# Attention loads on 128 and 96 partitions, and the second expert's lower parts on VectorE alone

## The chip, the cores and the metric

The kernel runs on one core of a Trainium2 chip. The metric is device microseconds of one execution. TensorE (PE) multiplies matrices from SBUF into PSUM, VectorE (DVE) and ScalarE (ACT) work element by element, GpSimd (POOL) does element work too and issues the gathers and scatters, and SyncE (SP) issues the plain loads and stores. All of these issue into the same 16 DMA engines. TensorE's clock is granted at one of two levels; the profile shows it as 1.00 (2.4 GHz) or 0.50 (1.2 GHz).

## The reference, cut to what matters

```
x = attention(q, k, v)             # 4 batches, 8 heads, 576 positions, head width 64, fp32
    # heads 0..3: a window of the last 32 positions
    # heads 4..7: the last 128 positions, every 4th of them
x = moe(x, ...)                    # 2304 rows of 512; 8 experts, each row goes to its best two
    # h = relu(x @ w1[e]); out += weight * (h @ w2[e]);  w1: 512x1024, w2: 1024x512
return moe2(x, ...)                # the same shapes, each row goes to its best expert
```

## The kernel before

**Attention.** The host has brought the heads into two halves: `half` 0 holds heads 0 to 3 on partitions 0 to 63 of q and k (head width on the partitions), `half` 1 heads 4 to 7 on partitions 64 to 127. Positions are cut into 9 blocks of 64 per half and batch. A "bank" is a pair of blocks: 4 pairs of half 1, one mixed pair of the two last blocks, 4 pairs of half 0, so 9 banks per batch and 36 in all. Loop L1030 does one bank per turn and is skewed: in turn i TensorE does the scores of bank i (L862), the values of bank i-2 (L909), the closing transposes of bank i-3 (L924) and the transposes of the probabilities of bank i-1 (L897). VectorE writes each bank's result to a tile `xo` (L921), of which there are 3; SyncE stores it to `x1` in DRAM (L938, L943). So `xo` of bank 3 can be written once the store of bank 0 has landed. v is held with 96 positions per block: 64 of its own on partitions 32 to 95 and the last 32 of the block before on partitions 0 to 31, each with a load of its own (`load_v`, L825).

SyncE issues all attention loads and stores in program order: batch 0 at L972, batch b+1 while batch b is worked on (L1064 to L1081), as loads of one half of q or k (64 partitions) each. Zeros for the array `x2`, into which the first MoE accumulates, are stored in three pieces in turns 22, 26 and 30 (L950, L1074).

**Weights.** Products of the MoE layers are made from a high part `whi` and a lower part `wlo` of every weight. `load_piece` (L184) loads 1 MB into `raw` (two buffers), ScalarE rounds it to `whi` (L208), and `wlo = raw - whi` (L209) is made in four instructions of 128x512: those with even number on VectorE, the others on the engine `eng`. `eng` is VectorE everywhere but for w1 and w2 of the second expert (L1292 with si = 0, L1268 with si = 1), where it is GpSimd. (The first expert's w1 is made by GpSimd alone, L1084.) While these run, VectorE also does the last part of the first routing (L992, L993), and `xh` and `xl`, the two parts of the second expert's 384 gathered rows (L711 on ScalarE, L712 on VectorE), in three steps from PSUM tiles t, x and q. TensorE's first product of the second expert needs all of `xh` and `whi`, its second all of `xl`.

Within attention the order on VectorE and ScalarE is as written; behind it the framework's scheduler sets it. TensorE's order is as written everywhere.

Of the kernel before, what the change touches and what calls it, by code (L numbers as in the profile page):

```python
# [7 lines left out]
F32 = mybir.dt.float32  # L8
# [9 lines left out]
P = 128  # L18
QB, KB = 64, 96
# [15 lines left out]
Z_AT = (22, 26, 30)  # L35
# [26 lines left out]
def attention_moe_moe_kernel(  # L62
# [5 lines left out]
    nc = tc.nc  # L68
    B, D2, H4, S = q.shape
    D, H = D2 // 2, 2 * H4  # L70
    N, DM = out.shape
    E, _, F = m1_w1.shape
# [139 lines left out]
    def load_w(ring, w, n_out, eng=nc.vector, cuts=1, after=None, all_on=None):  # L212

        ps = []
        per = 2048 // n_out
        for c in range(w.shape[0] // (per * P)):
            hi, lo = load_piece(ring, w[c * per * P:(c + 1) * per * P, :].rearrange("(c p) f -> p c f", p=P), eng, cuts, after, all_on)
            for u in range(per):
                ps.append((hi[:, u * n_out:(u + 1) * n_out], lo[:, u * n_out:(u + 1) * n_out]))
        return ps  # L220
# [575 lines left out]
    with ExitStack() as actx:  # L796
# [6 lines left out]
        KP = KB - QB  # L803
        qs = [ak.tile([P, HH, S], F32, name=f"q{i}") for i in range(2)]
        ks = [ak.tile([P, HH, KP + S], F32, name=f"k{i}") for i in range(2)]
        vs = [ak.tile([P, NB, HH * D], F32, name=f"v{i}") for i in range(3)]
        for k_ in ks:
            nc.vector.memset(k_[:, :, :KP], 0.0)
        for v_ in vs:
            nc.vector.memset(v_[:KP, 0], 0.0)  # L810
        zero = ak.tile([P, P], F32, name="zero")
        nc.vector.memset(zero, 0.0)

        def load_q(b, half, c0=0, c1=S):
            o = half * D
            return qs[b % 2][o:o + D, :, c0:c1], q[b, o:o + D, :, c0:c1]

        def load_k(b, half, c0=0, c1=S):
            o = half * D
            return ks[b % 2][o:o + D, :, KP + c0:KP + c1], k[b, o:o + D, :, c0:c1]  # L820

        def v_of(b, half):
            return vs[(2 * b + 1 - half) % 3]
# [1 line left out]
        def load_v(b, half, j0=0, j1=NB):  # L825

            vb = v_of(b, half)
            src = v[b, half].rearrange("(j p) d -> p j d", p=QB)
            f = max(j0, 1)
            return [(vb[KP:KB, j0:j1], src[:, j0:j1]),  # L830
                    (vb[:KP, f:j1], src[QB - KP:, f - 1:j1 - 1])]


        S4 = S // 4
# [110 lines left out]

        r1 = Route(2, E * cap1 // P, max(r for _, r in regs1), nat, late1)
        n_dyn1 = dyn_tiles(2 * N + sum(r for _, r in regs1), N + r1.pad, rows1)
        ZROWS = -(-(N + P) // (32 * len(Z_AT))) * 32

        def zeros(r0, n):  # L950
            return (x2[r0:r0 + n].rearrange("r d -> (r d)").rearrange("(p c d) -> p c d", p=P, d=P),
                    zero[:, None, :].to_broadcast([P, n * DM // P // P, P]))

        b_tiles = [(b + 1) * S // P for b in range(B)]
        last_pe, last_st = [None], [None]
# [1 line left out]
        def issue(loads):  # L957
            for dst, src in loads:
                nc.sync.dma_start(dst, src)
# [5 lines left out]
        def busy(n, after=None):  # L965

            with tc.issue_after(after) if after is not None else ExitStack():
                for _ in range(n):
                    nc.tensor.matmul(warm, one.to_broadcast([P, P]), one.to_broadcast([P, 224]), start=True, stop=True)

        busy(WARM)
        issue([load_k(0, 1, 0, KB), load_q(0, 1, 0, P), *load_v(0, 1, 0, 2), load_k(0, 1, KB, S), load_q(0, 1, P, S),  # L972
               *load_v(0, 1, 2), load_k(0, 0), load_q(0, 0), *load_v(0, 0)])
        for dst, a, b_ in ((wg1, m1_wg, m1_wn), (wg2, m2_wg, m2_wo)):
            nc.gpsimd.dma_start(dst[:, :, 0, :], a.rearrange("(c p) e -> p c e", p=P))
            nc.gpsimd.dma_start(dst[:, :, 1, :], b_.rearrange("(c p) e -> p c e", p=P))
# [53 lines left out]
        for i in range(len(all_banks) + to_f):  # L1030
            bi = i % n_bi
            if i < len(all_banks):
                bk = Bank()
                bk.b, bk.bi, bk.blocks = all_banks[i]
                queue.insert(0, bk)
                scores(bk)
                if i < len(WARM_1):
                    busy(WARM_1[i], last_pe[0])
            else:
                queue.insert(0, None)  # L1040
            if len(queue) > to_v and queue[to_v]:
                values(queue[to_v])
            if ready:
                logits_part(*ready.pop())
                go_on()
            if len(queue) > to_f:
                bk = queue.pop()
                if bk.bi == 0:
                    xT = ak.tile([P, DC, S], F32, name="xT")
                    if bk.b % 2 == 0:  # L1050
                        lgT = ak.tile([G, 2 * S], F32, name="lgT")
                bk.xT = xT
                finish(bk)
                half, j = bk.blocks[1]
                if half == 0:
                    c0, c1 = (j - 1) * QB, S if bk.bi == n_bi - 1 else (j + 1) * QB
                    ready.append((bk.b, c0, c1 - c0, xT, lgT))
            if len(queue) > to_t and queue[to_t]:
                transposes(queue[to_t])
            if i >= E0_AT and 0 in first_x:  # L1060
                first_products(E0_N)

            if i < len(all_banks):
                if bi == 0:  # L1064
                    more = [[] for _ in range(n_bi)]
                    b = i // n_bi + 1
                    if b < B:
                        for h in (1, 0):
                            f = 0 if h else 4
                            more[f].append(load_k(b, h))  # L1070
                            more[f + 1].append(load_q(b, h))
                            more[f + 2] += load_v(b, h, 0, 4)
                            more[f + 3] += load_v(b, h, 4)
                if i in Z_AT:  # L1074
                    z0 = Z_AT.index(i) * ZROWS
                    more[bi].append(zeros(z0, min(ZROWS, N + P - z0)))
                if last_st[0] is None:
                    issue(more[bi])
                else:
                    with tc.issue_after(last_st[0]):  # L1080
                        issue(more[bi])  # L1081
            if i == W1_AT:
                with tc.issue_after(last_st[0]):
                    w_1 = load_w(wr1, m1_w1[0], F, nc.gpsimd, 4, None, nc.gpsimd)  # L1084
# [163 lines left out]
    def w2_of(role):  # L1248
        if role not in by_load:
            return m1_w2[role]  # L1250
        return m1_w2[bass.ds(number[role], 1)].rearrange("a f d -> (a f) d")
# [10 lines left out]
    def experts1(si):  # L1262

        us = segs[si]
        e, loop = us[0][0], si == LOOP_AT
        w1, x0 = nxt["w1"], nxt["x"]
        if not loop:
            w2 = load_w(wr2, w2_of(e), DM, nc.gpsimd if si == 1 else nc.vector, cuts=4 if si in (0, len(segs) - 1) else 1)  # L1268
        left = Steps(rest() if si == 0 else rest_and_x(us))
        xs = [x0] + [left if si == 1 else Steps(seg_x(us, i)) for i in range(1, len(us))]  # L1270
        if si != 1:
            for x_ in xs[1:]:
                x_.take(99)
        held = []
        for ui, (_, n, early, a) in enumerate(us):
            if si == 0:
                h = nxt["h"].result
            elif ui == 0 and si == len(segs) - 1:
                h = mixed(mm1_steps(w1, x0, n), Steps(route2_logits(0, late2)), *MIX_ROUTE2[0])
                done(r2.part(*done(top_one(0, late2)), 0, late2, (0, reg2, 0)))  # L1280
            elif ui == 0 and si == 1:
                h = mixed(mm1_steps(w1, x0, n), left, *MIX_LEFT[1], False)
            else:
                h = mm1_unit(w1, x0 if ui == 0 else xs[ui].result, n)
            if loop and ui == 0:

                dyn_loop(r1, n_over1[0], 0, x1, m1_w1, m1_w2, True, x2)
                w2 = load_w(wr2, w2_of(e), DM)
            held.append((h, n, r1.idx_a[e] if early else r1.idx_f if e < n_fix else r1.idx, a))
            if ui == len(us) - 1:  # L1290
                if si + 1 < len(segs):
                    nxt["w1"] = load_w(wr1, w1_of(segs[si + 1][0][0]), F, nc.gpsimd if si == 0 else nc.vector)  # L1292
                    x_next = Steps(seg_x(segs[si + 1], 0))
                    if si > 0:
                        x_next.take(99)
                else:
                    start_moe2()
            if not loop or ui == len(us) - 1:
                for h, n, idx, a in held:
                    if ui == 0 and si < 2:  # L1300
                        mixed(mm2_steps(w2, h, n, idx, a, True, x2), left, *MIX_LEFT[2 * si], False)
                        while not (left.over if si else 1 in first_x):
                            left.take(1)
                    else:
                        mm2_unit(w2, h, n, idx, a, True, x2)
                held = []
        if si == 1:
            n_over1[0] = dyn_count(r1, 0, n_dyn1)
        if si + 1 < len(segs):
            x_next.take(99)  # L1310
            nxt["x"] = x_next.result
# [205 lines left out]
```

## Time and profile before

| | us |
|---|---|
| three timed runs | 892.93, 893.58, 896.59 (median 893.58) |
| profiled execution, its own time | 897.35 |
| its span, first to last instruction | 895.1 |
| TensorE busy | 846.1 (95% of the span) |
| VectorE busy | 455.4 (51%) |
| GpSimd busy | 239.1 (27%) |

The times are read from the start of the span. Attention takes the first 160 us or so, the first MoE layer follows up to about 650, then the second. In a row of a timeline, the bracket at the end is the idle time of the engine ahead of that instruction and what ended it.

### The profile page before, as it was taken

To read this page: it belongs to the slowest core of one execution; us is meant where nothing else is said; L and a number is where in the kernel's file an instruction comes from. 1 tells how busy PE (TensorE), PEld (TensorE's weight loads), DVE (VectorE), ACT (ScalarE), POOL (GpSimd) and SP (SyncE) were. 2 spreads that over 40 slices of the span, in tenths; PEclk is the share of its full clock that TensorE was granted. 3 is DMA by queue.
4 is the path that set the end of the run, shared out by engine and by line. 5 is a ranking of instruction groups with operands and counts; after the bars stand their busy time and mean duration, and the time that the engine had idled before them with its cause. 6 is when DMAs were issued, how large, how long until landed. Compare 5 with 4: busy or idle time off the path is not lost. (4 is left out here: it accounts for less than half of the span.)

```text
span 895.1 us, 15646 instructions
## 1 busy us (share of the span) xinstructions
PE 846.1 (95%) x5844; PEld 730.6 (82%) x5844; DVE 455.4 (51%) x1291; ACT 381.4 (43%) x991; POOL 239.1 (27%) x289
## 2 busy tenths in 40 slices
PE   8799999979999999999999999798999999999994
PEld 6677777868889899889898989786877989898883
DVE  2347688687426224652441616466454646545450
ACT  2446646441425324352442526323323545545451
POOL 5005243253312323232322422412214111221111
PEclk7789999989999999999999999999999999999997
DMA  8969874444327443554352814425543667454630
GB/s 188 203 177 251 237 215 118 132 116 148 57 47 263 117 124 84 173 163 122 86 192 28 265 24 133 119 58 151 116 153 97 217 223 241 165 186 154 212 116 16
DMA packets 77519, 131.83 MB, mean 147 GB/s; under 512 B 5977, under 2 KB 42153, under 8 KB 76992
## 3 DMA queue, kind: packets, MB, share of 16 engines
q1 hardware_dynamic: 64240, 97.27, 35.0%
q0 software_dynamic: 13200, 33.52, 16.1%
q8 instruction: 47, 0.77, 0.4%
q14 instruction: 32, 0.26, 0.1%
HBM read 106.86 MB, written 24.15 MB: 146 GB/s over the span
## 5 line engine op out<-in xcount | busy, mean ns | idle before, releaser
L209 DVE TENSOR_TENSOR wlo<-raw,whi 128x512 fp32r<-128x512 f32 x256 | 165.0, 701 | 123.4 <-ACT whi L208 123.2
L208 ACT CAST whi<-raw 128x512 fp32r<-128x512 f32 x264 | 144.3, 618 | 38.3 <-DMA raw<-in_moe_w_dram 13.0
L226 PE MATMUL a<-xh,whi 128*128 128x256 f32 (+13 forms) x368 | 113.8, 309 | 3.1 <-ACT xh L711 3.1
L226 PE MATMUL a<-xl,whi 128*128 128x256 f32 (+13 forms) x368 | 112.2, 305 | 2.6 <-DVE xl L712 2.6
L226 PE MATMUL a<-xh,wlo 128*128 128x256 f32 (+13 forms) x368 | 112.1, 305 | 2.0 <-issue 2.0
L226 PE MATMUL v<-xh,whi 128*128 128x256 f32 (+13 forms) x368 | 113.1, 307 | 0.0
L226 PE MATMUL v<-xl,whi 128*128 128x256 f32 (+13 forms) x368 | 111.4, 303 | 0.0
L226 PE MATMUL v<-xh,wlo 128*128 128x256 f32 (+13 forms) x368 | 111.3, 302 | 0.0
L226 PE MATMUL a<-whi,hl 128*128 128x512 f32 (+4 forms) x248 | 97.5, 393 | 0.0
L226 PE MATMUL a<-wlo,hh 128*128 128x512 f32 (+5 forms) x248 | 97.0, 392 | 0.0
L226 PE MATMUL a<-whi,hh 128*128 128x512 f32 (+4 forms) x240 | 95.2, 397 | 0.0
L226 PE MATMUL v<-whi,hl 128*128 128x512 f32 (+1 forms) x240 | 94.1, 392 | 0.0
L226 PE MATMUL v<-wlo,hh 128*128 128x512 f32 (+6 forms) x240 | 93.4, 393 | 0.0
L1114 POOL DMA_INDIRECT x_scratch<-y,sca x30 | 49.1, 1635 | 140.1 <-ACT y L1143 81.5
L226 PE MATMUL v<-whi,hh 128*128 128x512 f32 (+1 forms) x200 | 79.3, 397 | 0.0
L767 DVE SCALAR_TENSOR_TENSOR hl<-v,hh 128x256 fp32r<-128x256 f32 (+13 forms) x92 | 42.6, 463 | 69.3 <-ACT hh L766 69.1
L767 DVE SCALAR_TENSOR_TENSOR hl<-a,hh 128x256 fp32r<-128x256 f32 (+13 forms) x92 | 42.6, 463 | 66.3 <-ACT hh L766 66.1
L226 PEld LDWEIGHTS a<-xh,whi 128*128 128x128 f32 x368 | 70.7, 192 | 4.3 <-ACT xh L711 3.5
L226 PEld LDWEIGHTS a<-xl,whi 128*128 128x128 f32 x368 | 70.9, 193 | 3.5 <-DVE xl L712 2.8
L766 ACT ACTIVATE hh<-a 128x256 fp32r<-128x256 f32 (+13 forms) x92 | 38.4, 417 | 82.5 <-PE a L226 81.4
L766 ACT ACTIVATE hh<-v 128x256 fp32r<-128x256 f32 (+13 forms) x92 | 38.4, 417 | 81.0 <-PE v L226 80.7
L226 PEld LDWEIGHTS a<-xh,wlo 128*128 128x128 f32 x368 | 70.8, 192 | 2.3 <-issue 2.3
(376 smaller groups left out, 1558.2 us busy)
## 6 DMA issues: line engine op xcount, KB each, us to landing
raw<-in_moe_w_dram SPq DMA_DIRECT2D x60, 1024.0 KB
raw<-in_moe_w_dram SPq DMA_DIRECT2D x32, 256.0 KB
k<-in_k_dram SPq DMA_DIRECT2D x7, 576.0 KB
q<-in_q_dram SPq DMA_DIRECT2D x7, 576.0 KB
x_scratch<-zero SPq DMA_DIRECT2D x2, 1664.0 KB
x_nextscratch<-xo SPq DMA_DIRECT2D x20, 128.0 KB
v<-in_v_dram SPq DMA_DIRECT2D x6, 320.0 KB
v<-in_v_dram SPq DMA_DIRECT2D x7, 256.0 KB
```

The lines of the kernel that those rows point to most:

```text
L208: nc.scalar.copy(hi_, raw_)
L209: (nc.vector if i % 2 == 0 and all_on is None else eng).tensor_sub(lo_, raw_, hi_.bitcast(F32))
L226: r = op(*args, **kw)
L766: nc.scalar.activation(hh[:, f, :n], ph[:, :n], AF.Relu)
L767: nc.vector.scalar_tensor_tensor(hl[:, f, :n], ph[:, :n], 0.0, hh[:, f, :n].bitcast(F32), op0=ALU.max, op1=ALU.subtract)
L1114: nc.gpsimd.indirect_dma_start(out=dst, out_offset=bass.IndirectOffsetOnAxis(ap=idx, axis=0), in_=y, in_offset=None, compute_op=ALU.add)
```

## The change

Three edits. (1) In batch 0, k and q are loaded with 64 partitions for their first 128 positions of half 1, then with 128 partitions for the positions behind of both halves, then the first 128 positions of half 0; for later batches each of q and k is one load of 128 partitions, issued in turns 0 and 1 of the batch before, in place of four half loads in turns 0, 1, 4 and 5. v is one load of 96 partitions that reads overlapping rows, but for its first block. (2) The zeros are stored as rows of 2048 bytes from a tile of 128x512 in place of 512 bytes from 128x128. (3) `eng` is VectorE for the second expert too.

```diff
-        vs = [ak.tile([P, NB, HH * D], F32, name=f"v{i}") for i in range(3)]
+        vs = [ak.tile([KB, NB, HH * D], F32, name=f"v{i}") for i in range(3)]
-        zero = ak.tile([P, P], F32, name="zero")
+        zero = ak.tile([P, DM], F32, name="zero")
...
+        def load_q(b, half=None, c0=0, c1=S):
+            p = slice(0, P) if half is None else slice(half * D, (half + 1) * D)
+            return qs[b % 2][p, :, c0:c1], q[b, p, :, c0:c1]
...
-            return [(vb[KP:KB, j0:j1], src[:, j0:j1]),
-                    (vb[:KP, f:j1], src[QB - KP:, f - 1:j1 - 1])]
+            at_f = src[:, f:j1]
+            (step, _), *others = [list(x_) for x_ in at_f.ap]
+            return loads + [(vb[:, f:j1], bass.AP(at_f.tensor, at_f.offset - KP * step, [[step, KB], *others]))]
...
-        ZROWS = -(-(N + P) // (32 * len(Z_AT))) * 32
+        ZROWS = -(-(N + P) // (P * len(Z_AT))) * P
...
+            fills = [(x2[r0:r0 + m].rearrange("(p c) d -> p c d", p=P),
+                      zero[:, None, :].to_broadcast([P, m // P, DM]))]
...
-        issue([load_k(0, 1, 0, KB), load_q(0, 1, 0, P), *load_v(0, 1, 0, 2), load_k(0, 1, KB, S), load_q(0, 1, P, S),
-               *load_v(0, 1, 2), load_k(0, 0), load_q(0, 0), *load_v(0, 0)])
+        issue([load_k(0, 1, 0, P), load_q(0, 1, 0, P), *load_v(0, 1, 0, 2), load_k(0, None, P, S), load_q(0, None, P, S),
+               *load_v(0, 1, 2), load_k(0, 0, 0, P), load_q(0, 0, 0, P), *load_v(0, 0)])
...
+                        more[0].append(load_k(b))
+                        more[1].append(load_q(b))
                         for h in (1, 0):
-                            f = 0 if h else 4
-                            more[f].append(load_k(b, h))
-                            more[f + 1].append(load_q(b, h))
-                            more[f + 2] += load_v(b, h, 0, 4)
-                            more[f + 3] += load_v(b, h, 4)
+                            f = 2 if h else 6
+                            more[f] += load_v(b, h, 0, 4)
+                            more[f + 1] += load_v(b, h, 4)
...
-            w2 = load_w(wr2, w2_of(e), DM, nc.gpsimd if si == 1 else nc.vector, cuts=4 if si in (0, len(segs) - 1) else 1)
+            w2 = load_w(wr2, w2_of(e), DM, nc.vector, cuts=4 if si in (0, len(segs) - 1) else 1)
...
-                    nxt["w1"] = load_w(wr1, w1_of(segs[si + 1][0][0]), F, nc.gpsimd if si == 0 else nc.vector)
+                    nxt["w1"] = load_w(wr1, w1_of(segs[si + 1][0][0]), F, nc.vector)
```

On SyncE, at the start of the program, k_258 and q_256 belong to batch 0 and k_259 and q_257 to batch 1; v_260, v_261 and v_262 are the three v tiles. Before, from the sixth load (ahead of it stand k 64x4x96, q 64x4x128, v 64x2x256, v 32x256 and k 64x4x480) to the first store:

```order
L959 DMA q_256<-in_q_dram 64x4x448
L959 DMA v_260<-in_v_dram 64x7x256
L959 DMA v_260<-in_v_dram 32x7x256
L959 DMA k_258<-in_k_dram 64x4x576
L959 DMA q_256<-in_q_dram 64x2304
L959 DMA v_261<-in_v_dram 64x9x256
L959 DMA v_261<-in_v_dram 32x8x256
L959 DMA k_259<-in_k_dram 64x4x576
L959 DMA q_257<-in_q_dram 64x2304
L959 DMA v_262<-in_v_dram 64x4x256
L959 DMA v_262<-in_v_dram 32x3x256
L943 DMA x_nextscratch<-xo 128x256
```

On SyncE now, from the fifth load (ahead of it stand k 64x4x128, q 64x4x128, v 64x256 and v 96x256) to the first store:

```order
L967 DMA k_258<-in_k_dram 128x4x448
L967 DMA q_256<-in_q_dram 128x4x448
L967 DMA v_260<-in_v_dram 96x7x256
L967 DMA k_258<-in_k_dram 64x4x128
L967 DMA q_256<-in_q_dram 64x4x128
L967 DMA v_261<-in_v_dram 64x256
L967 DMA v_261<-in_v_dram 96x8x256
L967 DMA k_259<-in_k_dram 128x4x576
L967 DMA q_257<-in_q_dram 128x2304
L967 DMA v_262<-in_v_dram 64x256
L967 DMA v_262<-in_v_dram 96x3x256
L946 DMA x_nextscratch<-xo 128x256
```

Batch 0 is complete at the same place, but k and q of batch 1 now stand ahead of the first store with both halves, not one.

On VectorE, where the second expert's `xl` is made: wlo_2786 and wlo_2798 are the lower parts of its w1, wlo_2921 of its w2 (wlo_2773, wlo_2785 and wlo_2908 in the change). Before, the last rows up to the last third of `xl`:

```order
L712 TENSOR_TENSOR xl384_2823<-x_2888,xh384_2822 128x4x128
L209 TENSOR_TENSOR wlo_2798<-raw_2795,whi_2797 128x2x256
L257 TENSOR_TENSOR oh_2839<-eq_2876,f_2882 128x40
L317 TENSOR_TENSOR val_2972<-val_2972 128x5
L522 TENSOR_TENSOR wts_271<-oh_2839,val_2972 128x40
L209 TENSOR_TENSOR wlo_2798<-raw_2795,whi_2797 128x2x256
L469 TENSOR_TENSOR msum_2969<-oh_2839 128x40
L412 CAST w2h_3069<-val_2972 128x10
L414 TENSOR_TENSOR w2l_3071<-val_2972,w2h_3069 128x10
L712 TENSOR_TENSOR xl384_2823<-q_2906,xh384_2822 128x4x128
L209 TENSOR_TENSOR wlo_2921<-raw_2918,whi_2920 128x512 x2
```

On VectorE now, all rows from the first lower part of that w1 to the last third of `xl`:

```order
L209 TENSOR_TENSOR wlo_2773<-raw_2770,whi_2772 128x2x256 x4
L257 TENSOR_TENSOR oh_2826<-eq_2829,f_2838 128x40
L712 TENSOR_TENSOR xl384_2810<-t_2851,xh384_2809 128x4x128
L303 SCALAR_TENSOR_TENSOR nl_2821<-oh_2826,nl_2821 128x40
L712 TENSOR_TENSOR xl384_2810<-x_2875,xh384_2809 128x4x128
L209 TENSOR_TENSOR wlo_2785<-raw_2782,whi_2784 128x2x256 x4
L247 TENSOR_REDUCE mb_2849<-nl_2821 128x5
L712 TENSOR_TENSOR xl384_2810<-q_2893,xh384_2809 128x4x128
```

Four more lower parts stand ahead of the last third of `xl`, and twelve small routing instructions stand behind it that stood ahead of it. On ScalarE one instruction moves: the exponent `val<-dm` (L311), which waits for VectorE's routing, stands behind all three parts of `xh` and the result y, where it stood ahead of the second part.

On GpSimd, at the same place, `x_scratch<-y` are the scatters of the first expert's results. Before:

```order
L705 DMA xg<-x_nextscratch,gata_2629 128x512 x3
L1114 DMA x_scratch<-y,scaa_2061 2432x512
L209 TENSOR_TENSOR wlo<-raw,whi 128x2x256 x4
L1114 DMA x_scratch<-y,scaa_2061 2432x512
L209 TENSOR_TENSOR wlo<-raw,whi 128x512 x4
L573 IOTA thr 128x21
```

On GpSimd now:

```order
L705 DMA xg<-x_nextscratch,gata_2616 128x512 x3
L1122 DMA x_scratch<-y,scaa_2048 2432x512 x2
L573 IOTA thr 128x21
L583 IOTA ia 128x27
L705 DMA xg<-x_nextscratch,gatf 128x512
```

The eight lower parts are gone from GpSimd; nothing else moves there. TensorE's order is the same in both programs.

## Rows read from the trace of the kernel before

**Rows 1.** Timeline of TensorE: start us, us, what, count [idle before <-releaser]

```profile
12.16 1.55 PE L226 MATMUL a<-k,q 64*64 64x96 f32 x16 [1.65 <-DMA q<-in_q_dram]
...
29.55 0.45 PE L226 MATMUL v<-v,pT 96*64 96x64 f32 x8 [0.33 <-ACT pT L906]
...
30.90 0.88 PE L226 MATMUL a<-k,q 64*64 64x96 f32 x16
36.70 1.15 PE L226 MATMUL v<-v,pT 96*64 96x64 f32 x16 [4.92 <-DVE pT L904]
```

**Rows 2.** Timeline of VectorE and of SyncE, the first stores

```profile
35.89 0.42 DVE L921 TENSOR_TENSOR xo<-v,rs 128x256 f32<-128x256 f32 x1 [5.96 <-DMA x_nextscratch<-xo]
...
21.13 0.36 SPq L943 DMA_DIRECT2D x_nextscratch<-xo  x1
```

**Rows 3.** Timeline of TensorE, later scores, and one later wait

```profile
53.64 0.88 PE L226 MATMUL a<-k,q 64*64 64x96 f32 x16
...
57.01 0.88 PE L226 MATMUL a<-k,q 64*64 64x96 f32 x16
...
71.29 0.88 PE L226 MATMUL a<-k,q 64*64 64x96 f32 x16
...
79.65 0.88 PE L226 MATMUL a<-k,q 64*64 64x96 f32 x16
...
106.41 0.91 PE L226 MATMUL v<-v,pT 96*64 96x64 f32 x16 [1.26 <-DVE pT L904]
```

**Rows 4.** Windows: stretch, length, busy us per engine; last PEclk, DMA share, GB/s

```profile
16.00:19.00 3.00, 3.00 (x25) 2.15 (x24) 1.34 (x5) 0.51 (x3) 2.28 (x3) 0.50 0.96 192
22.00:30.00 8.00, 7.67 (x112) 6.06 (x113) 4.54 (x17) 4.83 (x23) 0.00 (x0) 0.99 1.08 155
36.00:52.00 16.00, 15.30 (x140) 12.12 (x141) 7.42 (x25) 8.20 (x41) 0.00 (x0) 0.50 0.82 208
68.00:70.00 2.00, 1.49 (x28) 1.07 (x28) 1.84 (x6) 1.89 (x11) 1.92 (x3) 1.00 1.05 360
108.00:114.00 6.00, 6.00 (x59) 4.58 (x59) 5.13 (x27) 3.94 (x22) 1.41 (x4) 0.50 0.99 308
186.00:192.00 6.00, 3.85 (x12) 3.85 (x13) 5.90 (x9) 2.18 (x4) 4.87 (x4) 0.50 0.58 181
211.00:215.00 4.00, 4.00 (x22) 3.36 (x21) 3.73 (x18) 0.69 (x1) 0.65 (x2) 1.00 1.02 419
```

**Rows 5.** Timeline of TensorE at the second expert's first products

```profile
185.13 0.44 PE L226 MATMUL a<-xh,whi 128*128 128x384 f32 x1 [3.07 <-ACT xh L711]
188.15 0.69 PE L226 MATMUL a<-xl,whi 128*128 128x384 f32 x1 [2.58 <-DVE xl L712]
```

**Rows 6.** Timeline of ScalarE ahead of them

```profile
181.84 0.21 ACT L311 ACTIVATE val<-dm 128x5 f32<-128x5 f32 x1 [3.37 <-DVE dm L310]
...
182.42 2.18 ACT L208 CAST whi<-raw 128x512 fp32r<-128x512 f32 x4
184.50 0.58 ACT L711 CAST xh<-q 128x512 fp32r<-128x512 f32 x1
```

**Rows 7.** Timeline of VectorE ahead of them

```profile
176.81 0.69 DVE L209 TENSOR_TENSOR wlo<-raw,whi 128x512 fp32r<-128x512 f32 x1
177.42 3.08 DVE L257 TENSOR_TENSOR oh<-eq,f 128x40 f32<-128x40 f32 x1
...
183.86 1.27 DVE L257 TENSOR_TENSOR oh<-eq,f 128x40 f32<-128x40 f32 x1
...
187.41 0.69 DVE L712 TENSOR_TENSOR xl<-q,xh 128x512 fp32r<-128x512 f32 x1
188.01 4.18 DVE L209 TENSOR_TENSOR wlo<-raw,whi 128x512 fp32r<-128x512 f32 x2
```

**Rows 8.** Timeline of GpSimd beside them

```profile
177.29 3.14 POOL L209 TENSOR_TENSOR wlo<-raw,whi 128x512 fp32r<-128x512 f32 x2
183.63 2.66 POOL L209 TENSOR_TENSOR wlo<-raw,whi 128x512 fp32r<-128x512 f32 x2 [3.21 <-ACT whi L208]
```

More of the change, by code (lines that the diff above doesn't have):

```diff
@@ L810, in attention_moe_moe_kernel, with load_k @@
             nc.vector.memset(v_[:KP, 0], 0.0)
-        zero = ak.tile([P, P], F32, name="zero")
+        zero = ak.tile([P, DM], F32, name="zero")
         nc.vector.memset(zero, 0.0)
[L814 to L820, printed above, removed]
+        def load_q(b, half=None, c0=0, c1=S):
+            p = slice(0, P) if half is None else slice(half * D, (half + 1) * D)
+            return qs[b % 2][p, :, c0:c1], q[b, p, :, c0:c1]
+        def load_k(b, half=None, c0=0, c1=S):
+            p = slice(0, P) if half is None else slice(half * D, (half + 1) * D)
+            return ks[b % 2][p, :, KP + c0:KP + c1], k[b, p, :, c0:c1]
         def v_of(b, half):
@@ L828, in load_v @@
             src = v[b, half].rearrange("(j p) d -> p j d", p=QB)
+            loads = [(vb[KP:KB, :1], src[:, :1])] if j0 == 0 else []
             f = max(j0, 1)
-            return [(vb[KP:KB, j0:j1], src[:, j0:j1]),
-                    (vb[:KP, f:j1], src[QB - KP:, f - 1:j1 - 1])]
+            at_f = src[:, f:j1]
+            (step, _), *others = [list(x_) for x_ in at_f.ap]
+            return loads + [(vb[:, f:j1], bass.AP(at_f.tensor, at_f.offset - KP * step, [[step, KB], *others]))]
         S4 = S // 4
@@ L947, in attention_moe_moe_kernel @@
         n_dyn1 = dyn_tiles(2 * N + sum(r for _, r in regs1), N + r1.pad, rows1)
-        ZROWS = -(-(N + P) // (32 * len(Z_AT))) * 32
+        ZROWS = -(-(N + P) // (P * len(Z_AT))) * P
         def zeros(r0, n):
-            return (x2[r0:r0 + n].rearrange("r d -> (r d)").rearrange("(p c d) -> p c d", p=P, d=P),
-                    zero[:, None, :].to_broadcast([P, n * DM // P // P, P]))
+            m = n // P * P
+            fills = [(x2[r0:r0 + m].rearrange("(p c) d -> p c d", p=P),
+                      zero[:, None, :].to_broadcast([P, m // P, DM]))]
+            if n > m:
+                fills.append((x2[r0 + m:r0 + n], zero[:n - m]))
+            return fills
         b_tiles = [(b + 1) * S // P for b in range(B)]
@@ L1067, in attention_moe_moe_kernel @@
                     if b < B:
+                        more[0].append(load_k(b))
+                        more[1].append(load_q(b))
                         for h in (1, 0):
-                            f = 0 if h else 4
-                            more[f].append(load_k(b, h))
-                            more[f + 1].append(load_q(b, h))
-                            more[f + 2] += load_v(b, h, 0, 4)
-                            more[f + 3] += load_v(b, h, 4)
+                            f = 2 if h else 6
+                            more[f] += load_v(b, h, 0, 4)
+                            more[f + 1] += load_v(b, h, 4)
                 if i in Z_AT:
                     z0 = Z_AT.index(i) * ZROWS
-                    more[bi].append(zeros(z0, min(ZROWS, N + P - z0)))
+                    more[bi] += zeros(z0, min(ZROWS, N + P - z0))
                 if last_st[0] is None:
```

## The prediction

> **What bounds the kernel now.** I read the page first. TensorE is busy for 846.1 of 895.1 us, so time can come only from its few idle places, from its clock, and from what makes it idle. Then I read TensorE's timeline around the idle places near the two edits, the timelines of the engines that end these waits, and windows for the granted clock and the DMA rate.
>
> Place one is the start. Bank 1's scores wait for q and begin at 12.16 [rows 1].
>
> Place two is the first store. VectorE wants to write bank 3's `xo` at about 29.9 (values done at 30.00) and can do so at 35.89, after 5.96 us of waiting for bank 0's store to land [rows 2]. SyncE had issued that store at 21.13, so it spent some 14 us behind the loads in the queues. TensorE idles for 4.92 us of this wait [rows 1], and then works at the half clock: the stretch from 36 to 52 shows 0.50, the one from 22 to 30 shows 0.99 [rows 4]. So the wait is paid for twice.
>
> Place three is the second expert's start. Its first product waits 3.07 us for `xh`, its second 2.58 us for `xl` [rows 5], and the stretch from 186 to 192 again runs at 0.50 with 3.85 us busy of 6 [rows 4].
>
> The sum is made against the profiled execution, 897.35 us (span 895.1 and 2.25 around it). That is 3.8 above the median of 893.58, so I take the difference over to the median.
>
> **Part 1a, the loads up to bank 1.** Bytes follow from the shapes. Ahead of bank 1's q, the small loads are 0.39 MB before and 0.43 MB now. Behind them before come 0.95 MB to 64 partitions, and now 1.84 MB to 128 partitions. A q load to 64 partitions alone moved 192 GB/s; loads to 128 partitions moved 360 (rows of 1 KB) and 419 (rows of 4 KB) [rows 4]. Before: 0.95 MB at 192 is 4.95 us, so the small loads ended at about 7.2. Now: 4.4 to 5.1 us for the 1.84 MB and 0.1 to 0.2 more for the small ones, so q lands at 11.7 to 12.5. That is ±0.4 against 12.16, and I take 0. If the rate did not rise at all, q would land at about 16.9.
>
> **Part 1b, the first store.** Ahead of it now stand 2.26 MB up to bank 1's q and another 4.52 MB, 6.78 MB in all (before 5.60), since batch 1's k and q come with both halves. The 4.52 MB at 360 GB/s take 12.6 us, so they end at 24.8 by rate alone. Three things are added. The stretch from 22 to 30 moved only 155 GB/s, while GpSimd's small gate loads (L975 to L977) were in the queues; against the 208 of 36 to 52 [rows 4] that is 8 us × 53 GB/s = 0.42 MB, some 2 us, and I keep it in full. The v loads to 96 partitions have no row: they are as fast as those to 128 partitions, or their first 64 go at 192 GB/s. For 1.77 MB of v and 0.39 MB of loads still cut to 64 partitions the second bound is 6.1 + 2.0 us against 6.0, +2.2; the loads follow one another in queues, so that others can use the engines that are free, and I take half, 1.1. And the same reckoning misses the old store by a little: 4.26 MB behind q's landing at 192 to 208 GB/s take 20.5 to 22.2 us, with 2 for the slow stretch to 34.6 to 36.3, and it landed at 35.8 (`xo` goes on at 35.89); the lag is up to 1.2. So the new store lands between 26.8 (no more than the slow stretch) and 30.2, some 28.5, and 33 if the lag is of the order of the slow stretch and more. It is wanted at 29.9, and TensorE has about 1 us of slack against VectorE here (5.96 against 4.92).
>
> What is it worth? From bank 6's scores (30.90, the last before the wait) to bank 10's (53.64 [rows 3]) pass 22.74 us for four banks. At full clock with nothing late, three intervals took 8.36 from 71.29 to 79.65, 2.79 each, and one took 3.37 from 53.64 to 57.01 [rows 3]. 3 × 2.79 + 3.37 = 11.74, so at most 11.0 is lost here. I take -10.5, leaving 0.5 of waiting. The condition is that TensorE's idle time stays small: the clock fell in the stretch 108 to 114 [rows 4] behind an idle time of only 1.26 us at 105 to 106.4 [rows 3]. If about 2 us stay and the clock falls, what remains is -3.6 to -7 (4.92 of idle less 1.3, up to that and half of the clock's cost of 6.1). If the store is as late as now, 0; if it is later, the other side, below.
>
> The Trainium skill, on the page "SBUF — State Buffer", section "Door 1: The DMA port swizzle (why [64,N] ≈ [32,N])", has a rule that speaks against my rate. Partitions 0 to 63 reach 8 of 16 ports (196 GB/s measured for 1 MiB), all 128 reach 16 ports (328 GB/s), and in a load of 96 partitions the even ports would carry twice what the odd ones do. By 328, q would land some 0.5 us later and the store some 2 us later, near 30.5. The trace agrees on the 64 partitions (192) and shows more than the page on 128 (360 and 419 [rows 4]), so I stay with 360.
>
> **Part 2, the zeros.** 2432 rows of 2 KB replace 9728 of 512 bytes. No engine waits for these stores in any row I read; cost 0. The bigger memset (128x512) is on VectorE ahead of its first work, where it waits for loads. If that cover were gone it costs less than the 0.69 us of a 128x512 operation [rows 7].
>
> **Part 3, the lower parts on VectorE.** It adds eight L209 of 0.69 us (0.61 from start to start, 176.81 to 177.42 [rows 7]) for the two pieces, four of them ahead of the last `xl`. It removes GpSimd's, two of which took 3.14 and 2.66 us [rows 8]. What the rows show beside them: VectorE's 128x40 operation L257 takes 3.08 us from 177.42, beside GpSimd's pair from 177.29, ending with it; another takes 1.27 at 183.86 beside the next pair; and two of its own L209 take 4.18 from 188.01 [rows 7, 8]. A 128x40 operation is a small fraction of a 128x512 one of 0.69, so I put 0.2 for it. GpSimd's work thus holds VectorE up. On the same path ScalarE waits 3.37 us for `dm` at 181.84, with two casts (2.18 for four) and the last `xh` behind it [rows 6].
>
> I re-time the new order from these rows. Four L209 from 176.81 to 179.25; L257 and `xl` of t to 180.1; `xl` of x to 180.85; ScalarE's casts, no longer behind `val<-dm`, from 179.4 to 181.5, and `xh` of q at 182.0; four L209 as casts come, to 183.3; L247; `xl` of q 183.45 to 184.1. TensorE's second product then starts at 184.15, not 188.15: -4.0. Best: TensorE never idles long enough to lose the clock, up to 3.4 more from the stretch 186 to 192, -7.4. Worst: the long durations are VectorE's own, and four more L209 only add 4 × 0.61 = +2.4. I take -4.0, since the first pair and L257 begin and end together (180.43 and 180.50). The four of w2 stand behind and are wanted only at the products with w2: cost 0, hidden by the products with w1; if that cover is gone, 2.4. GpSimd's scatters come earlier, and nobody waits for them.
>
> TensorE's order is the same in both programs and it is the bound behind these places, so what is gained is kept to the end. Sum: 0 - 10.5 + 0 - 4.0 = -14.5: 882.9 against the profiled 897.35, 879.1 against the median.
>
> **The rivals.** Rival 1: the store still comes late enough for TensorE to idle about 2 us, and the clock falls for part of the stretch. For it: 1.26 us was enough once; the slow stretch and the 96-partition loads may both cost more than I put. Against: the bytes halve in time. -3.6 to -7 and -4.0: 882.5 to 886, say 885.
>
> Rival 2: GpSimd's work is not what holds VectorE. Attention gains 10.5, the expert loses 0 to 2.4: 883 to 885.5. Those rows speak against it.
>
> Rival 3, the slower side: loads run no faster on 128 partitions, because a queue, not the partitions, sets 192. Then all loads ahead of bank 1's q (+4.7) and ahead of the store (1.18 MB more at 200, +5.9) come later, with the clock as low as now; less 4.0 it is +6.6: 900. It decides from a rate under about 240 GB/s (6.78 MB against 5.60 at 200). Against it stand 360 and 419 in the same trace; for it, that those are other loads, with other row lengths.
>
> Rival 4: the store lands as late as now, since small loads in the queues decide it and not bytes, and VectorE's gain is given back at the casts: 0 to -3, 890.5 to 893.6. For it: 155 GB/s in the slow stretch; ahead of the store stands more, not less.
>
> **How the numbers follow.** Forecast 61%, Rival 1 17%, Rival 2 8%, Rival 3 6%, Rival 4 8%. The forecast's own range is 874 (best case at the expert, 3.4 more, and 1 to 2 from the start) to 883. Low end for all 871, high end 890: that leaves out Rivals 3 and 4 and a little below. About 0.5%, here 4.5 us, is what a measurement of this kernel can tell from no change. Faster by more than that, under 889.1: forecast, Rivals 1 and 2, less a little for sizes, 0.83. Within it: Rival 4 and that little, 0.11. Slower, over 898.0: Rival 3, 0.06.
>
> **What would show it.** The windows of attention's first loads above 300 GB/s, and bank 1's scores near 12. `xo` of bank 3 without a wait of over 1 us, the stretch from 36 to 52 at 1.00, and bank 10's scores about 11 us earlier. L257 at 0.2 us, and TensorE's waits for `xh` and `xl` at some 2 us together where they were 5.65. Wrong would be: a half clock that stays behind bank 6, L257 as long as now with GpSimd idle, or bank 1 starting past 14.

## The result, and the profile after

The changed kernel takes 884.68 us in the median of four executions (883.02, 884.33, 885.03 and one of 2195.31 that no row explains), against 893.25 for the kernel before in the same runs: ratio 0.9894, interval [0.9863, 0.9925]. A second measurement, below, gives 0.9864 [0.9832, 0.9895]. The ratios count only executions within 1.5% of the fastest of their kernel: that of 2195.31 is out, and further down three of nine of the changed kernel, with which its second measurement would be 0.990, and two of six each in e8 and e9. So the change is worth 1.0 to 1.4%, some 9 to 12 us, where 14.5 were forecast. The profiled execution took 885.03 (span 883.3). Line numbers in rows are those of each run's own kernel: L924, L922 or L928 is the L921 of the kernel before, and so on.

TensorE in the profile after, timeline rows (start, length, what, idle before): the scores of banks 1, 6 and 10, the values of bank 4, which wait, and the second expert's second product.

```profile
11.31 0.88 PE L226 MATMUL a<-k,q 64*64 64x96 f32 x16 [2.42 <-DMA q<-in_q_dram]
...
25.57 0.88 PE L226 MATMUL a<-k,q 64*64 64x96 f32 x16
31.28 1.15 PE L226 MATMUL v<-v,pT 96*64 96x64 f32 x16 [4.83 <-DVE pT L907]
...
48.32 0.88 PE L226 MATMUL a<-k,q 64*64 64x96 f32 x16
...
178.61 0.44 PE L226 MATMUL a<-xl,whi 128*128 128x384 f32 x1 [1.28 <-DVE xl L712]
...
255.44 0.43 PE L226 MATMUL a<-xh,wlo 128*128 128x360 f32 x1 [2.03 <-issue]
```

Against [rows 1, 3, 5] of the kernel before, bank 1 begins 0.85 earlier (12.16), bank 6 already 5.33 earlier (30.90), bank 10 still 5.32 (53.64), and the second product of the expert 9.54 (188.15). The row at 255.44 has its like in the kernel before at 266.63, so the gap is 11.2 there, and 11.8 at the end:

```profile
266.63 0.43 PE L226 MATMUL a<-xh,wlo 128*128 128x360 f32 x1 [2.04 <-issue]
```

Two places gained, then: the stretch from bank 1 to bank 6, and the second expert. The place on which the forecast rested, between bank 6 and bank 10, gave nothing: TensorE idles for 4.83 us there as it did for 4.92.

VectorE after, rows that answer to [rows 2, 7]:

```profile
30.48 0.42 DVE L924 TENSOR_TENSOR xo<-v,rs 128x256 f32<-128x256 f32 x1 [5.87 <-DMA x_nextscratch<-xo]
...
171.53 2.50 DVE L209 TENSOR_TENSOR wlo<-raw,whi 128x512 fp32r<-128x512 f32 x4
173.94 0.20 DVE L257 TENSOR_TENSOR oh<-eq,f 128x40 f32<-128x40 f32 x1
...
177.87 0.68 DVE L712 TENSOR_TENSOR xl<-q,xh 128x512 fp32r<-128x512 f32 x1
```

The wait for the first store is 5.87 us, as long as before (5.96): it ends 5.4 us earlier, and it begins 5.3 us earlier too. At the expert four L209 take 2.50 us and L257 behind them 0.20, where it took 3.08 [rows 7].

Windows of the profile after (stretch, length, busy us of PE, PEld, DVE, ACT, POOL; granted clock, DMA share, GB/s):

```profile
14.00:17.00 3.00, 3.00 (x49) 2.36 (x47) 1.79 (x6) 2.12 (x13) 1.26 (x2) 1.00 1.11 239
18.50:20.00 1.50, 1.50 (x15) 1.02 (x12) 0.89 (x3) 1.50 (x9) 1.50 (x2) 1.00 1.02 390
22.00:30.00 8.00, 4.12 (x61) 3.08 (x59) 1.91 (x7) 4.03 (x21) 0.00 (x0) 1.00 0.99 248
31.00:47.00 16.00, 15.72 (x141) 12.26 (x141) 7.00 (x24) 8.26 (x41) 0.00 (x0) 0.50 0.52 159
180.00:186.00 6.00, 6.00 (x36) 6.00 (x35) 4.01 (x9) 3.93 (x8) 0.00 (x0) 1.00 0.72 198
```

k and q to 128 partitions move at 390 GB/s (18.5 to 20), as forecast; v to 96 partitions, alone in the queues from 14 to 17, moves at 239. The clock at the start is 1.00 now, where [rows 4] had 0.50, and 0.50 behind the wait as before. At the second expert it stays at 1.00 (180 to 186; [rows 4] 0.50).

Single executions of a kernel spread here over 8 to 22 us (the kernel before from 889.30 to 902.96 in one set of runs; only e10 stays within 4), and a profile shows one of them; verdicts below go by the ratios, causes by the rows.

### The profile page after: what moved, and what is told of

The parts are those of the page before. It is cut to its first block, busy times and chain, and to the rows that moved or that the text cites. A ratio compares the mean times of both kernels' runs of the same rounds, so it can differ in the third digit from the quotient of the medians.

```text
span 883.3 us, 15626 instructions
## 1 busy us (share of the span) xinstructions
PE 840.0 (95%) x5844; PEld 725.8 (82%) x5844; DVE 450.1 (51%) x1299; ACT 380.9 (43%) x991; POOL 227.5 (26%) x281
## 5 line engine op out<-in xcount | busy, mean ns | idle before, releaser
L209 DVE TENSOR_TENSOR wlo<-raw,whi 128x512 fp32r<-128x512 f32 x264 | 165.9, 686 | 126.5 <-ACT whi L208 125.7
```

Source lines behind the costliest of these rows:

```text
L209: (nc.vector if i % 2 == 0 and all_on is None else eng).tensor_sub(lo_, raw_, hi_.bitcast(F32))
```

## The experiments

**The third edit alone (e1, this diff on the kernel before), and the changed kernel without it (e2, the same lines turned back).**

```diff
-            w2 = load_w(wr2, w2_of(e), DM, nc.gpsimd if si == 1 else nc.vector, cuts=4 if si in (0, len(segs) - 1) else 1)
+            w2 = load_w(wr2, w2_of(e), DM, nc.vector, cuts=4 if si in (0, len(segs) - 1) else 1)
-                    nxt["w1"] = load_w(wr1, w1_of(segs[si + 1][0][0]), F, nc.gpsimd if si == 0 else nc.vector)
+                    nxt["w1"] = load_w(wr1, w1_of(segs[si + 1][0][0]), F, nc.vector)
```

> The kernel before with only the third edit (all lower parts of the second expert on VectorE). Theory A (the gain at the second expert is its own, GpSimd's work beside VectorE made the waits for xl): -5 to -6.5 against the kernel before, 887 to 888.5; L257 at about 0.2 us, TensorE's wait for xh gone, that for xl under 1.5 us, no half clock behind it; the start as before: half clock from about 12 to 22 and bank 6's scores near 30.9. Rival B (the whole gain comes from attention): within 1.5 of the kernel before. Theory C (the half clock of the first 22 us is chance of one execution): the start differs from the profile of before though nothing is changed there.

> The changed kernel with the third edit undone (GpSimd takes its share of the second expert's lower parts again). Theory A: only the attention gain stays, -3 to -5.3 against the kernel before, 888 to 890; start as in the changed kernel (bank 6's scores near 25.6, clock 1.00 up to there), a wait of about 5.9 us for the first store, and at the second expert L257 near 3 us and waits of 5.6 us in sum on TensorE. Rival B: 884 to 886, as the changed kernel. If the gain of the start is chance of the execution: 891 to 893.

Measured: e1 887.42 against 894.41, ratio 0.9935 [0.9906, 0.9963]; e2 890.22, ratio 0.9979 [0.9950, 1.0008]. The second expert alone brings 0.65%, probably the larger part. The other two edits alone bring 0.2%, not clear of nothing (e2). On top of the third they bring 0.4 to 0.7% (the changed kernel's 0.9894 and 0.9864 against e1's 0.9935), but 0.2% by the medians of all executions (885.19 of 894.18 against 887.42 of 894.41). For the expert theory A holds. In e1 TensorE's second product there waits 1.02 us for `xl`, and the clock stays at 1.00 behind it. In e2, with GpSimd's share back, both waits of the kernel before are back, and so is the long L257 (VectorE, then TensorE):

```profile
166.12 3.44 DVE L257 TENSOR_TENSOR oh<-eq,f 128x40 f32<-128x40 f32 x1
```
```profile
174.19 0.44 PE L226 MATMUL a<-xh,whi 128*128 128x384 f32 x1 [3.07 <-ACT xh L711]
177.21 0.69 PE L226 MATMUL a<-xl,whi 128*128 128x384 f32 x1 [2.57 <-DVE xl L712]
```

From bank 10 to this second product pass 134.5 us in the kernel before and 134.8 in e2, 130.3 in the changed kernel and 130.2 in e1. For the start theory C holds: e1 has the loads of the kernel before, and its start looks like this (TensorE, then VectorE).

```profile
26.18 0.88 PE L226 MATMUL a<-k,q 64*64 64x96 f32 x16
34.25 1.15 PE L226 MATMUL v<-v,pT 96*64 96x64 f32 x16 [7.20 <-DVE pT L904]
...
51.53 0.88 PE L226 MATMUL a<-k,q 64*64 64x96 f32 x16
```
```profile
33.45 0.42 DVE L921 TENSOR_TENSOR xo<-v,rs 128x256 f32<-128x256 f32 x1 [8.23 <-DMA x_nextscratch<-xo]
```

Bank 6 at 26.18 with the old loads, not at 30.90: the half clock from 12 to 22 in the profile of before was one execution's. At full clock the old loads make the wait longer, 8.23 us, and bank 10 comes at 51.53, not 53.64. In e2, with the new loads, it was the other way about, and not as theory A had it: half clock at the start, and a wait of only 2.08.

**The changed kernel again.** No edit.

> The changed kernel once more, to compare with the others of this call and to see a second execution of its start. The two profiled executions with its attention loads differ: one keeps the full clock up to 30 us and then waits 5.87 us for the first store, the other (without the third edit) has the half clock from 11 to 21 and then waits 2.08. Theory C2 (which of the two comes is chance of the execution, the landing of the store is not): 884 to 888, the store ends its wait at 30.4 to 31.2 whichever clock the start has. Rival F (the start at full clock belongs to the changed kernel): bank 6's scores again at 25.6, wait 5.9.

Measured: 885.19 against 894.18, ratio 0.9864 [0.9832, 0.9895]. Its profiled execution took 879.85; TensorE, VectorE and windows:

```profile
12.03 1.55 PE L226 MATMUL a<-k,q 64*64 64x96 f32 x16 [4.24 <-DMA q<-in_q_dram]
...
30.52 0.88 PE L226 MATMUL a<-k,q 64*64 64x96 f32 x16
31.75 0.91 PE L226 MATMUL v<-v,pT 96*64 96x64 f32 x16 [0.36 <-DVE pT L907]
...
42.18 0.88 PE L226 MATMUL a<-k,q 64*64 64x96 f32 x16
```
```profile
30.95 0.42 DVE L924 TENSOR_TENSOR xo<-v,rs 128x256 f32<-128x256 f32 x1 [1.40 <-DMA x_nextscratch<-xo]
```
```profile
12.00:21.00 9.00, 8.97 (x72) 7.02 (x73) 2.55 (x8) 3.75 (x21) 4.79 (x7) 0.50 1.11 258
22.00:30.00 8.00, 7.67 (x111) 6.06 (x108) 4.43 (x16) 5.21 (x26) 0.00 (x0) 1.00 1.03 271
31.00:47.00 16.00, 15.44 (x238) 12.09 (x235) 10.72 (x35) 10.79 (x54) 0.00 (x0) 1.00 0.72 233
```

This is the execution that the forecast describes: half clock at the start, as in the profile of before, a store that comes just in time, 1.00 from 31 to 47, and bank 10 at 42.18, 11.5 us earlier than [rows 3]. C2 holds: the wait ends at 30.48 and 30.95 in the two executions (31.18 in e2), whatever clock the start has, and only what TensorE has done by then differs. With the old loads its end is less steady: 35.89 in the kernel before, 33.45 in e1, 33.51 in e11. So the new loads bring it 2.3 to 5.4 us earlier.

**GpSimd beside VectorE again.** In the loads of the second expert's w1 and w2 (`beside[0]` is true there) GpSimd makes a subtraction that nobody reads (e6; the lines that set `beside` are left out).

```diff
+            if beside[0] and i % 2 == 1:
+                nc.gpsimd.tensor_sub(raw_, raw_, hi_.bitcast(F32))
```

> The changed kernel, and GpSimd does one more subtraction of 128x512 behind every second lower part of the second expert's w1 and w2 (raw minus whi into raw, which nobody reads), eight in all, so that it works beside VectorE as it did before. VectorE's order up to xl is that of the changed kernel. Theory A (GpSimd's work beside VectorE lengthens VectorE's instructions): xl's last part comes 2 to 4 us later, some of the L209, L257 or L712 near 175 to 179 last two to five times as long, +2 to +6 against the changed kernel. Rival E (the order and ScalarE's wait for the routing made the waits, not GpSimd): within 1 of the changed kernel, VectorE's durations unchanged.

Measured: 889.71 against 894.41, ratio 0.9941 [0.9909, 0.9973]; so by the ratios 0.5 to 0.8% of the change's 1.1 to 1.4% are lost again (the interval overlaps that of its first measurement, and is clear of the second's). VectorE and TensorE:

```profile
171.33 3.59 DVE L211 TENSOR_TENSOR wlo<-raw,whi 128x512 fp32r<-128x512 f32 x4
...
176.87 3.55 DVE L211 TENSOR_TENSOR wlo<-raw,whi 128x512 fp32r<-128x512 f32 x4
180.34 0.18 DVE L251 TENSOR_REDUCE mb<-nl 128x5 f32<-128x40 f32 x1
180.44 0.68 DVE L716 TENSOR_TENSOR xl<-q,xh 128x512 fp32r<-128x512 f32 x1
```
```profile
181.17 0.69 PE L230 MATMUL a<-xl,whi 128*128 128x384 f32 x1 [3.78 <-DVE xl L716]
```

The same VectorE instructions in the same order up to `xl`: four lower parts now take 3.59 and 3.55 us, not 2.50, and the wait for `xl` is 3.78, not 1.28; the product behind it takes 0.69, which is the half clock (0.44 at the full one). For `xl` theory A holds, and E falls as its cause. The stretch was less than two to five times, 1.4 for the four together. The wait for `xh` did not come back (its product follows without idle time at 176.95), and L257, which has no GpSimd row beside it here, kept its 0.19 us: how much of the old wait for `xh` came from GpSimd and how much from the place of `val<-dm` on ScalarE, e6 does not tell.

**The wait for the store, taken away in three ways.** e4 issues batch b+1's k and q in turns 3 and 4 and v in turns 5 to 7. e3 and e5 give `xo` five buffers, in the changed kernel and in the one before (second part of the diff).

```diff
-                        more[0].append(load_k(b))
-                        more[1].append(load_q(b))
+                        more[3].append(load_k(b))
+                        more[4].append(load_q(b))
-                            f = 2 if h else 6
+                            f = 5 if h else 6
...
+        ao = actx.enter_context(tc.tile_pool(name="ao", bufs=5))
-            bk.xo = at.tile([P, HH, D], F32, name="xo")
+            bk.xo = ao.tile([P, HH, D], F32, name="xo")
```

> The changed kernel with batch b+1's loads of k and q issued in turns 3 and 4 of batch b and of v in turns 5 to 7, so that 3.2 MB (k, q and v of batch 1) no longer stand ahead of the first store. Theory A (the first store is late because of the bytes ahead of it): it lands near 21 us, the wait of 5.87 us at xo is gone and the clock stays at 1.00 from 30 to 48; -8 to -10.5 against the changed kernel, 874 to 877. Rival D (a wait only moves: later stores, or bank 9's scores for the later loads of batch 1): -4 to +2 against the changed kernel, with a wait of some us at a later xo or at bank 9's k or q.

> The changed kernel with xo in a pool of its own with 5 buffers in place of 3, so that bank 3 and 4 wait for no store; all loads and stores as in the changed kernel. Theory A (the wait for the store and the half clock behind it are what the forecast lacks): no wait over 1 us at xo, clock 1.00 from 30 to 48 where the start had it, -4 to -9 against the changed kernel, 876 to 881. Rival D (the wait moves to bank 5's xo or to another resource): -2 to +1.

> The kernel before with xo in a pool of its own with 5 buffers. Theory A: the 5.96 to 8.23 us wait at bank 3 goes, what is left is a shorter one at bank 5 (whose xo is wanted some 5 us later): -5 to -10 against the kernel before, 884 to 889, so that the narrow loads cost little once nobody waits for their store. Rival G (the loads themselves are late: batch 0's half 0 or batch 1's half 1 then becomes the wait): -3 to 0.

Measured: e4 880.28, ratio 0.9845 [0.9799, 0.9891]; e3 877.81, 0.9822 [0.9794, 0.9850]; e5 883.48, 0.9870 [0.9848, 0.9892]. In none of the three profiles does VectorE wait for the store; bank 3's `xo` in e4, e3 and e5:

```profile
28.74 0.42 DVE L924 TENSOR_TENSOR xo<-v,rs 128x256 f32<-128x256 f32 x1
...
26.41 0.42 DVE L925 TENSOR_TENSOR xo<-v,rs 128x256 f32<-128x256 f32 x1
...
34.47 0.42 DVE L922 TENSOR_TENSOR xo<-v,rs 128x256 f32<-128x256 f32 x1
```

e5's profile is of an execution of 895.27 us that runs at the half clock from 12 to 55, so it does not show the new buffers beside a start at full clock. Five buffers are worth as much in the kernel before as the whole change: theory A for e5, with no wait left at bank 5 either. On top of the change they bring some 0.4% (e3 against the second measurement of the changed kernel, in the same runs; the intervals overlap), or 0.8% by the medians of all executions (877.81 against 885.19). e4 brings no more that is clear, and less than theory A put. The gains do not add up: e5's 0.9870 times e1's 0.9935 is 0.9806, and e3, which has the new loads besides, stands at 0.9822. With five buffers the new loads thus bring nothing that can be told.

**A shorter wait at the start.** On e4, the 128-partition loads of k and q are cut at position 384.

```diff
-        issue([load_k(0, 1, 0, P), load_q(0, 1, 0, P), *load_v(0, 1, 0, 2), load_k(0, None, P, S), load_q(0, None, P, S),
-               *load_v(0, 1, 2), load_k(0, 0, 0, P), load_q(0, 0, 0, P), *load_v(0, 0)])
+        issue([load_k(0, 1, 0, P), load_q(0, 1, 0, P), *load_v(0, 1, 0, 2), load_k(0, None, P, 3 * P), load_q(0, None, P, 3 * P),
+               load_k(0, None, 3 * P, S), load_q(0, None, 3 * P, S), *load_v(0, 1, 2), load_k(0, 0, 0, P), load_q(0, 0, 0, P), *load_v(0, 0)])
```

> The kernel with the first store ahead of batch 1's loads (turns 3 to 7), and the 128-partition loads of batch 0's k and q cut at position 384, so that bank 1 waits for 1.05 MB of k and q behind the small loads and not for 1.84 MB. Theory H (the wait ahead of bank 1 is bytes at about 390 GB/s, and its length decides whether the clock falls at the start): bank 1 begins near 9.5 to 10, with idle of 2 us or less in place of 2.4 to 4.9, clock 1.00 from 10 to 22 in most executions; -2 to -6 against the uncut one (880), 874 to 878. Rival: bank 2 or 3 waits in its place for the second part or for v, 0 to -1.

Measured: 879.49 (873.83 to 893.43), 0.9803 [0.9764, 0.9843], against 0.9845 for e4 in other runs: inconclusive on the time. Bank 1 began at 9.65, as expected. But in the profiled execution (893.43) two microseconds of idle time were followed by the half clock, against theory H:

```profile
9.65 0.88 PE L226 MATMUL a<-k,q 64*64 64x96 f32 x16 [2.00 <-DMA q<-in_q_dram]
```
```profile
12.00:22.00 10.00, 10.00 (x86) 7.33 (x86) 3.65 (x12) 4.58 (x27) 4.78 (x7) 0.50 1.08 211
22.00:30.00 8.00, 8.00 (x52) 5.85 (x52) 2.25 (x7) 3.66 (x17) 0.00 (x0) 0.50 0.80 271
31.00:51.00 20.00, 20.00 (x181) 15.58 (x180) 8.70 (x29) 10.15 (x51) 0.00 (x0) 0.50 0.41 117
```

TensorE is busy without a gap from 12 to 51 and stays at 0.50.

**Idle products in the wait at the start.** 40 in place of 4 products L977 behind bank 0, in the changed kernel (e9) and in the one with five `xo` (e10).

```diff
-WARM_1 = (4, 8, 8)
+WARM_1 = (40, 8, 8)
```

> The changed kernel with 40 in place of 4 of the idle products (L977) behind bank 0, some 4 us of them, in the time in which TensorE waits for bank 1's q. Theory J (the store lands near 30.5 whatever the start does, so a start at full clock only lengthens the wait for it): the start keeps 1.00 in most executions, bank 6's scores near 25.5, the wait at xo 5 to 6 us and the half clock behind it as in the first profile of the changed kernel; 883 to 886, within 2 of the changed kernel. Rival K (the start's clock is what the changed kernel still loses): -3 to -6, 879 to 882.

> The kernel with five xo buffers and the same 40 idle products. Theory J: here the start's clock is kept and nobody waits for the store, so the fill is worth what the half clock at the start costs without it (1.7 to 5): 873 to 876 against 878 without the fill. Rival L (the clock falls by chance whatever TensorE does): within 1 of 878, with a half clock before 22 us in the profile.

Measured: e9 883.15 (874.99 to 891.55), 0.9860 [0.9818, 0.9903]; e10 872.29 (870.87 to 874.60), 0.9715 [0.9685, 0.9745]. With a store that somebody waits for the fill changes nothing that can be told. That is theory J's time, but its one profile does not show theory J's picture: it has a half clock from 14 to 21 all the same, and a wait for the store of 1.17 us. Where nobody waits the fill brings 1% (against e3, in other runs; 873 to 876 were expected), and rival L falls. The spread of the executions shrinks to 4 us, and their mean granted clock goes from between 0.972 and 0.983 (e3) to between 0.983 and 0.993, so the clock has a large part in it. This kernel is faster than the kernel before and than the changed one. Windows of its first 47 us:

```profile
12.00:22.00 10.00, 8.47 (x120) 6.94 (x121) 4.70 (x15) 5.25 (x31) 4.78 (x7) 1.00 1.11 272
22.00:30.00 8.00, 7.67 (x114) 6.07 (x111) 4.66 (x17) 5.42 (x28) 0.00 (x0) 1.00 1.02 264
31.00:47.00 16.00, 15.58 (x229) 12.20 (x229) 10.00 (x34) 10.82 (x54) 0.00 (x0) 1.00 0.80 262
```

**The zeros alone** (the second edit on the kernel before; the diff is that of the change).

> The kernel before with only the second edit (zeros stored as rows of 2048 bytes from a tile of 128x512). Theory A: nobody waits for these stores, within 1 of the kernel before. Rival: the fewer packets free the queues between 95 and 125 us, where the weights of the first expert are loaded, -1.5 to -4.

Measured: 897.58 against 896.43, ratio 1.0002 [0.9976, 1.0028]. Nothing, as forecast.

**v by two loads again**, in the changed kernel (e12):

```diff
-            loads = [(vb[KP:KB, :1], src[:, :1])] if j0 == 0 else []
             f = max(j0, 1)
-            at_f = src[:, f:j1]
-            (step, _), *others = [list(x_) for x_ in at_f.ap]
-            return loads + [(vb[:, f:j1], bass.AP(at_f.tensor, at_f.offset - KP * step, [[step, KB], *others]))]
+            return [(vb[KP:KB, j0:j1], src[:, j0:j1]),
+                    (vb[:KP, f:j1], src[QB - KP:, f - 1:j1 - 1])]
```

> The changed kernel with v loaded as before, by two loads of 64 and 32 partitions. In the changed kernel v to 96 partitions moved at about 245 GB/s, k and q to 128 at about 390. Theory M (a load is as slow as its first 64 partitions): v now at 200 to 220 GB/s, the first store lands 1 to 2 us later than the 30.4 to 31.2 of the changed kernel, 0 to +3 in time. Rival: v to 96 partitions brings nothing, the store lands at the same time.

Measured: 879.95 against 896.43, ratio 0.9797 [0.9754, 0.9839]. Both expectations were wrong: the old v loads, beside k and q on 128 partitions, are the faster ones. Windows in the middle of a v load (14 to 16), over the whole of it (13.4 to 16.2) and while k is loaded (17 to 19), then the whole of the same v load in the changed kernel, and bank 3's `xo` in e12:

```profile
14.00:16.00 2.00, 2.00 (x20) 1.67 (x21) 0.61 (x2) 0.51 (x3) 0.55 (x1) 0.50 1.10 351
13.40:16.20 2.80, 2.80 (x24) 1.93 (x22) 1.09 (x4) 1.11 (x7) 0.75 (x1) 0.50 1.11 312
17.00:19.00 2.00, 2.00 (x22) 1.72 (x21) 0.43 (x1) 0.91 (x6) 2.00 (x4) 0.50 1.04 394
```
```profile
13.70:17.40 3.70, 3.70 (x61) 3.01 (x61) 2.10 (x7) 2.76 (x16) 1.66 (x2) 1.00 1.11 240
```
```profile
27.87 0.42 DVE L922 TENSOR_TENSOR xo<-v,rs 128x256 f32<-128x256 f32 x1 [0.48 <-PE x L226]
```

Over the whole load 312 GB/s against 240, though the two loads read no fewer bytes. The first store, issued at 18.62, landed 9.1 us later by the list of DMA issues, at 27.7, three us before that of the changed kernel. This execution had a half clock from some 13 to 19, and `xo` was wanted at 27.4; wanted at 24.6, it would have waited for this store too. The interval just touches that of the changed kernel (0.9832 to 0.9895), so some 0.2 to 1% that the change leaves on the table is likely, not proved.

## Why the prediction was right in its range and wrong in its sum

The range held, but it had been stretched for the rivals: 884.7 lies outside the forecast's own 874 to 883. That the total came within 6 us of 879.1 is partly luck, since the largest term of the sum did not come as put and the expert gave more than its term.

Part 1a held in the middle: bank 1 begins between 11.05 (e12) and 12.81 (e4) in the profiles with the new loads uncut and no fill, and between 10.87 (e11) and 12.16 (before) with the old ones, though that is a wider scatter than the ±0.4 given. Part 2 held (e11).

The step that failed is part 1b, the wait for the first store put down as gone, -10.5. The rate of 390 and 394 for 128 partitions was right. Two sizes were not. First, the landing: 28.5 was put, 30.5 to 31.2 came. The difference is v to 96 partitions, for which 1.1 of a bound of 2.2 us was taken, from 192 GB/s for two thirds of its bytes. That bound is 288 GB/s for the whole load; measured were 240, slower than the bound, and e12, with v at 312, lands its store at 27.7, 2.8 us before the changed kernel's earliest. Second, the time at which it is wanted: 29.9 was read from one execution whose start ran at the half clock. At full clock it is wanted at about 24.6 (25.2 with the old loads). So the wait is 1.2 to 2.1 us in the three executions with some 7 us or more of half clock at the start (e9, the changed kernel again, e2), 3.91 in one with half as much (e6) and 5.87 in the one without, and each of the five has a half clock at the start or behind the wait. Over many executions attention's edits bring 0.2% by themselves (e2; the interval goes from a gain of 0.5 to a loss of 0.1) and 0.2 to 0.7% on top of the third edit: 2 to 6 us in place of 10.5.

The comparison had the same fault on its other side: 22.74 us from bank 6 to bank 10 were right for the execution shown, but other executions of the old loads reach bank 10 at 51.5 (e1) and 52.0 (e11). That the forecast's own picture exists is shown by the second profile of the changed kernel, 879.85.

Part 3 was right in mechanism and a little small: -4.0 was put, -5.8 [-8.4, -3.3] came (e1; the interval holds -4.0). Up to the second product the rows give 4.2 to 4.3, as put; the rest is the half clock behind it, which went too, since the wait for `xl` fell to 1.0 to 1.3 us, and which I had kept for the best case. `xh` waits no more. e6 shows that GpSimd's work beside VectorE makes the wait for `xl`; for `xh` it leaves the cause open.

Rival 1 (a store still late, a clock that falls behind it, 885) comes nearest, in the time and in its mechanism, and the 96-partition loads are among the reasons given for it; its 3.6 to 7 us for attention are more than e2 measured (1.9), and reach into what the changed kernel has on top of e1 (some 2 to 6). Rivals 2 to 4 fell: 2 by e1 and e6, 3 by 390 GB/s, 4 by the landing.

Open is what decides which clock the start gets. Idle time ahead of it does not by itself: 2.42 us were followed by 1.00 (the changed kernel), 2.00 by some forty us of half clock (e8), 1.58 by 1.00 (e10) and 1.65 by 1.00 for a microsecond or two and then the half clock (e9).

## What to carry to other kernels

A wait is the difference of two times, and the one at which the thing is wanted has to be looked up as carefully as the one at which it comes; a profile gives both for one execution only, and a granted clock in it can move the first by 5 us. Where an output buffer waits for a store behind prefetches, try more buffers first: two more took the wait away here, and brought the kernel before as much as the whole change did. When loads are widened, check each width: 128 partitions went at twice the rate of 64, 96 did not.

## What the runs showed of the hardware

- v to 96 partitions moved at 240 GB/s, the same bytes to 64 (partitions 32 to 95) and 32 partitions at 312, k and q to 128 at 390 to 394. The Trainium skill, page "SBUF — State Buffer", section "Door 1: The DMA port swizzle (why [64,N] ≈ [32,N])", has partitions 0 to 63 on the even ports alone and 64 and above on the odd ones, so that 0 to 95 put two thirds on the even ports and 32 to 95 put half on each. That agrees with 96 partitions being slower than 128. Two thirds of the bytes at the 192 GB/s of 64 partitions [rows 4] make an estimate of 288 for either form, since the bytes of each port are the same: the two loads come somewhat above it, and the one load stays below it. Why it does was not tried.
- With work on GpSimd beside it, four 128x512 subtractions of VectorE took 3.59 us in place of 2.50, and a 128x40 one 3.08 (e2: 3.44) in place of 0.20.
- TensorE was busy without a gap for 39 us at the half clock (e8), and idle times of nearly the same length were followed by it in one execution and not in another (e9, e10).
